# A ninth shared pair of chunks, a fifth weight buffer, and other orders at the ends of chunks, in an attention and mixture-of-experts kernel

## The chip, the cores and the metric

The kernel runs on one core of a Trainium2 chip. The metric is device time in microseconds (us) of one execution. The kernel before was timed three times: 1831.97, 1837.50 and 1835.14, median 1835.14.

## The reference

An attention without softmax over 8 batches of 2496 rows, with a product by `u`, feeds a mixture of eight experts with a gate for each row:

```python
scores = scale * np.matmul(z, z.transpose(0, 2, 1))   # z: 8 x 2496 x 64, scale = 1/2496
attn = np.maximum(scores, 0.0) ** 2
out = np.matmul(attn, v)                              # v: 8 x 2496 x 256
x = (u * out).reshape(19968, 256)
do_compute = x @ w_skip > 0                           # rows that go to an expert
e_idx = np.argmax(xc @ w_gate, axis=1)                # xc = x[do_compute]; 8 experts
h = np.maximum(xc[mask] @ w1[e], 0.0)                 # 256 -> 1024
y[mask] = gate_w[mask, None] * (h @ w2[e])            # 1024 -> 256
out[do_compute] = xc + y                              # all other rows: x
```

Queries and keys are the same `z`, so the matrix `attn` is symmetric.

## The kernel before

**Attention.** The queries of a batch are cut into five chunks c = 0 to 4: four of 512 and one of 448. The keys are cut into ten pairs of blocks p = 0 to 9, 256 keys each; p belongs to the key chunk j = p // 2. A step is one (chunk, p): 8 x 5 x 10 = 400 steps. In a step PE forms the scores of 256 keys against the chunk (L251, three products of two halves that run side by side on 64 rows of the array), ACT takes relu and square into the tile `r` (L290, L291), `high()` rounds `r` to `ah` (L313, on ACT where `on_act` says so, else on DVE), `low()` puts the rest into `al` on DVE (L317), and PE adds `ah`·`vh`, `ah`·`vl`, `al`·`vh` into four accumulators (`attend`, L341): `acc[d][t]` for the two halves d of the 256 columns and the two row halves t. Stages run two steps ahead (`LA = 2`).

**Shared weights.** `PAIRS` names chunk pairs (c, j), c < j. Chunk c computes the weights of j's keys, DVE transposes them in blocks (L268), and SP's queue writes them to memory (`keep`, L686). Chunk j later does not compute the weights of c's keys: SP's queue brings them back (`recall`, L280, issued five steps ahead), and only `high()` and `low()` remain. Such a step is "known" below. Batch 0 leaves out the pairs with c = 0. `ORDER[c]` sets the order of p within a chunk, `EXTRA[c]` which further p have their rounding on ACT.

**The end of a chunk.** In the last step (`k == NP - 1`) the accumulators of d = 0 are finished first; then come the products of the step before for d = 1, and its own. `part(d, 1)` copies `acc[d][1]` on ACT (L369), `part(d, 0)` adds `acc[d][0]` to it on DVE (L371); only then can the next chunk use those buffers, since `ps_acc` has four. `mul` (L374) multiplies by `u`, `turn_rows` (L378) transposes, `store` (L387) writes. After every second chunk `routing` computes logits on PE (`gates`, L409), transposes them (`logits`, L431, L435), picks the expert on DVE (`route`, `counts`), counts places on PE (`place`, L476) and writes each row's entry into its expert's list with an indirect DMA on GpSimd (POOL; `put_in`, L500).

**Loads.** `load_v` and `load_z` bring the next batch's `v` and `z` and split them on ACT and DVE (L119/L120, L108/L109) at steps set by `later(...)`; in the last three chunks `load_w` does it for expert 0.

**Experts.** After the attention each expert's rows run in units of 256. A unit has four `h_part`s (L598, then relu on ACT, L603, and the rest on DVE, L604) and then `y_part`s (L617). `fills` puts other work behind the k-th of these seven parts: 0 to 3 are the `h_part`s, 4 to 6 the `y_part`s. The first unit of expert 0 (its rows were fetched early) carries the routing of the last chunk in its fills: `logits` and `route` behind part 1, `counts` behind 2, `end_routes` (`place` and two `put_in`) behind 3, `end_lists` behind 5.

The order on each engine is that in which the code is written (`manual_schedule`): every engine's queue runs in that order and waits at an instruction whose inputs are not there.

Of the kernel before, what the change touches and what calls it, by code (L numbers as in the profile page):

```python
# [8 lines left out]
F32 = mybir.dt.float32  # L9
# [8 lines left out]
P = 128  # L18
# [7 lines left out]

PAIRS = ((0, 1), (0, 2), (0, 3), (1, 2), (1, 3), (2, 3), (2, 4), (3, 4))
ORDER = (  # L30
# [5 lines left out]
)  # L36
EXTRA = ((8,), (3, 8), (4, 5), (6, 7), (1, 3))


C_TRI, C_REV, C_OFF, C_IDS, C_THR, C_END = 0, 128, 192, 256, 260, 270  # L40
# [7 lines left out]
def attn_moe(ctx, tc, zT, uT, v, wg, w1, w2, cst, pad, out):  # L48
# [113 lines left out]

    def load_u(ci):
        b, q0, n = chunks[ci]
        uts[ci] = xp.tile([P, 2, QC], F32, name="ut", tag="ut", bufs=4)
        nc.sync.dma_start(uts[ci][:, :, :n], uT[b, :, :, q0 : q0 + n])

    warm = cpool.tile([P, 1], F32, name="warm")
# [83 lines left out]
        return ps  # L252

    def r_tile():
        return ap.tile([P, 2, QC], F32, name="r", tag="r", bufs=4)

    turned_r, puts, step = {}, [], [0]

# [135 lines left out]
    def routing(cis, rows64=True):  # L394
# [27 lines left out]
        def logits():  # L422

            ps = psg.pop()
            lgf = lg.rearrange("p t c -> p (t c)")
            same = all(n % P == 0 for n in ns)
            for g, n in [(0, ns[0])] if same else enumerate(ns):
                full = 32 * (n // P)
                w = P * len(ns) if same else P
                o = g * P  # L430
                nc.vector.transpose(lgf[:full, o : o + w], ps[:full, o : o + w])  # L431
                if n % P:
                    k = o + n % P
                    nc.gpsimd.memset(lgf[full : full + 32, k : o + P], 0.0)
                    nc.vector.transpose(lgf[full : full + 32, o:k], ps[full : full + 32, o:k])  # L435

        def route():
# [231 lines left out]
    def at(s, f):  # L669

        todo.setdefault(s // 2, []).append(f)
# [30 lines left out]
    for ci, (b, q0, n) in enumerate(chunks):  # L702
        s0 = ci * NB
        if ci + 1 < NC:
            at(s0 + 12, lambda ci=ci: load_u(ci + 1))
        if ci == 0:
            first = [(4 * j - 8, j % 2, 3, load_z, j) for j in range(2, NZ)]
            first += [(2 * g - 4, 1, 4, load_v, g) for g in range(2, NB // 2)]
            for s1, _, k, load, j in sorted(first, key=lambda x: x[:2]):
                eng = nc.vector  # L710
                if s1 - k < 0:
                    at(s1, load(0, j, eng))
                else:
                    later(s1 - k, k, load, 0, j, eng)
            at(14, lay_pads)
        if q0 == 0 and b + 1 < B:

            end = s0 + NB * -(-S // QC)
            for j in range(NZ):
                s1 = (s0 + 24, s0 + 44, end - 18, end - 14, end - 10)[j]  # L720
                later(s1, 7, load_z, b + 1, j, nc.vector)
            for g in range(NB // 2):
                s1 = s0 + 21 + 8 * g if g < 7 else (end - 17, end - 14, end - 12)[g - 7]
                later(s1, 7, load_v, b + 1, g, nc.vector)

    s_end = NC * NB
    s_w = s_end - 3 * NB

    def start_w():
        for k, f in enumerate(load_w(0, nc.vector)):  # L730
            at(s_w + 8 + 5 * k, f)

    at(s_w, start_w)

# [20 lines left out]
    for s, (ci, p) in enumerate(steps):  # L755
        b, q0, n = chunks[ci]
        k = s % NP
        step[0] = s
        ahead(s + LA + 3)
        if k == 0:  # L760
            accs[ci] = [[ps_acc.tile([P, QC], F32, name="acc", tag="acc") for _ in range(2)] for _ in range(2)]
        acc = accs[ci]
        if k < NP - 1:
            high, low = stage(s + LA)
            high()
            low()
            for d in range(2 if k < NP - 2 else 1):
                attend(b, n, p, d, acc[d], *aa[s], k == 0, False)
            if k < NP - 2:
                aa.pop(s)  # L770
        else:


            part, mul, rows0, rows1, store = finish(ci)
            attend(b, n, p, 0, acc[0], *aa[s], False, True)
            part(0, 1, acc[0])
            part(0, 0, acc[0])
            high, low = stage(s + LA)
            attend(b, n, steps[s - 1][1], 1, acc[1], *aa.pop(s - 1), False, False)
            if s + LA in known:  # L780

                high()
                low()
                high = low = lambda: None
            attend(b, n, p, 1, acc[1], *aa.pop(s), False, True)
            part(1, 1, acc[1])
            high()
            part(1, 0, acc[1])
            low()
            mul()  # L790
            accs.pop(ci)

            new.append(ci)
            if ci < NC - 1:
                after = [(rows0, 2), (rows1, 3), (store, 4), (store, 5)]
                if ci % 2 == 0:
                    gates, logits, route, counts, gate, place, put_in = routing(new)
                    after = [(gates, 2), (logits, 2), (rows0, 2), (rows1, 3), (route, 4), (counts, 4),
                             (store, 4), (gate, 5), (store, 5), (place, 6)]
                    for t in range(0, 4 * len(new), 2):  # L800
                        f = lambda put_in=put_in, t=t: put_in(t, t + 2)
                        if s + 6 + t < len(steps):
                            after.append((f, 6 + t))
                        else:
                            left.append(f)
                    new = []
                for f, k in after:
                    todo.setdefault(s + k, []).append(f)
            else:
                gates, logits, route, counts, gate, place, put_in = routing(new, False)  # L810
        for f in todo.pop(s, []):
            f()
        put_some()
# [57 lines left out]
    for e in range(E):  # L871
# [3 lines left out]
        for i in range(NFIX):  # L875
# [11 lines left out]
            elif i == 0:  # L887
                add(fills, (0, lambda: turn_pe(pair(0, 1), turned(0, 1))))
                add(fills, (0, gates), (0, rows0), (0, rows1), (0, store), (0, store), (1, logits), (1, route),
                    (2, counts), (2, gate), (3, end_routes), (5, end_lists))  # L890
                add(fills, *zip((0, 2), left))
            elif i == 1:
                add(fills, (1, end_counts), (3, lambda: turn_pe(pair(0, 2), turned(0, 2))), (4, rows(0, 3)), (6, rows(0, 4)))
                add(fills, *zip((1, 3, 5), wq[:3]))
            else:
                add(fills, (1, rows(1, 0)), (3, rows(0, 5)), (4, lambda: turn_pe(pair(0, 3), turned(0, 3))),
                    (5, rows(1, 1)), (6, lambda: load_ids(idts[2], 2, 2 * NSTAT)))
                add(fills, *zip((1, 2, 3, 5, 6), wq[3:]))
# [99 lines left out]
```

## Time and profile before

| | |
|---|---|
| median of three runs | 1835.14 us |
| the profiled execution: its own time, and its span | 1834.64 us, 1832.8 us |
| mean granted TensorE clock | 0.996 |
| attention | start to about 1322 us |
| experts | about 1322 us to the end |
| scores: matmuls of 448 columns (L251) | three groups x96 |
| scores: matmuls of 512 columns (L251) | three groups x460 |
| POOL's fill of logits (L434) | x8, 147 to 199 ns |

The span is from the first to the last instruction on the chip; the execution's own time has 1.8 us more around it. In a row of a timeline the first two numbers are the start and the duration in us; what stands in brackets is the idle time of the engine before it and who ended it. A group's row has the busy time in us and the mean ns of one instruction, then the idle time ahead of it.

### The profile page before, as it was taken

How to read it: one execution, taken by the hardware profiler on the slowest of the kernel's cores; microseconds unless marked ns; L12 is line 12 of the kernel's file. 1: busy time of each engine (PE TensorE's matmuls, PEld its weight loads, DVE VectorE, ACT ScalarE, POOL GpSimd, SP SyncE). 2: the span in 40 equal slices, each digit the busy share in tenths (PEclk: the TensorE clock that was granted, in tenths of full speed). 3: DMA queues.
4: the chain of work that ended last, by engine and by line, in shares of the span. 5: the costliest groups of instructions: out<-in, count | busy, mean ns of one | idle time of the engine just before them, and what ended most of it. 6: DMA issues, size and time to landing. Idle time of an engine off the chain costs nothing. (4 is left out here: it accounts for less than half of the span.)

```text
span 1832.8 us, 40463 instructions
## 1 busy us (share of the span) xinstructions
PE 1787.2 (98%) x15844; PEld 1575.9 (86%) x15844; DVE 1182.8 (65%) x2105; ACT 1159.5 (63%) x1499; POOL 440.8 (24%) x429
## 2 busy tenths in 40 slices
PE   8999999999999999999999999999989999999997
PEld 7888878877887798788879878877889999999997
DVE  6777776876777687678678777867643343334432
ACT  8877876877777687678777876877523233333321
POOL 0102201210220120121012022112254556635621
PEclk9999999999999999999999999999989999999999
DMA  5575687487657847784784787578542233313210
GB/s 185 128 179 138 168 207 190 122 207 187 170 136 196 207 116 193 202 198 119 186 215 108 183 208 187 133 182 197 147 103 76 80 96 106 89 53 94 84 37 26
DMA packets 403766, 267.46 MB, mean 146 GB/s; under 512 B 205859, under 2 KB 334117, under 8 KB 403440
## 3 DMA queue, kind: packets, MB, share of 16 engines
q1 hardware_dynamic: 389440, 240.47, 51.9%
q0 software_dynamic: 13712, 22.99, 4.4%
q8 instruction: 141, 2.31, 0.5%
q14 instruction: 185, 1.52, 0.3%
q10 hardware_dynamic: 288, 0.17, 0.0%
HBM read 145.80 MB, written 118.39 MB: 144 GB/s over the span
## 5 line engine op out<-in xcount | busy, mean ns | idle before, releaser
L341 PE MATMUL acc<-ah,vh 64*128 64x512 f32 (+1 forms) x3120 | 729.5, 387 | 17.5 <-DVE xrow L371 11.4
L341 PE MATMUL acc<-ah,vl 64*128 64x512 f32 (+1 forms) x3120 | 712.7, 385 | 0.0
L317 DVE TENSOR_TENSOR al<-r,ah 128x1024 fp32r<-128x1024 f32 (+3 forms) x464 | 480.0, 1048 | 251.1 <-ACT ah L313 238.8
L341 PE MATMUL acc<-al,vh 64*128 64x512 f32 (+1 forms) x3120 | 562.0, 385 | 3.6 <-DVE al L317 3.2
L341 PEld LDWEIGHTS acc<-ah,vh 64*128 64x128 f32 x3120 | 423.8, 185 | 87.4 <-DVE xrow L371 25.8
L341 PEld LDWEIGHTS acc<-ah,vl 64*128 64x128 f32 x3120 | 424.0, 185 | 45.9 <-DVE vl L120 0.2
L500 POOL DMA_INDIRECT lst<-pair,dest x160 | 192.4, 1203 | 1093.4 <-DVE dest L498 996.1
L290 ACT ACTIVATE r<-ps 128x1024 f32<-128x1024 f32 (+1 forms) x278 | 280.3, 1008 | 225.2 <-PE ps L251 185.3
L341 PEld LDWEIGHTS acc<-al,vh 64*128 64x128 f32 x3120 | 361.3, 185 | 58.6 <-DVE al L317 11.9
L313 ACT CAST ah<-r 128x1024 fp32r<-128x1024 f32 (+3 forms) x381 | 329.1, 891 | 37.8 <-DMA r<-kept 13.2
L291 ACT ACTIVATE r<-r 128x1024 f32<-128x1024 f32 (+1 forms) x278 | 289.9, 1043 | 8.8
L603 ACT ACTIVATE hh<-psh 128x512 fp32r<-128x512 f32 (+1 forms) x172 | 98.7, 584 | 293.2 <-PE psh L598 256.7
L617 PE MATMUL y<-w2t,hh 128*128 128x256 f32 x1328 | 246.5, 287 | 0.0
L598 PE MATMUL psh<-xt,w1h 128*128 128x256 f32 (+1 forms) x1280 | 231.8, 284 | 2.1 <-issue 1.8
L617 PEld LDWEIGHTS y<-w2t,hh 128*128 128x128 f32 x1328 | 208.7, 193 | 1.3 <-issue 1.3
L598 PEld LDWEIGHTS psh<-xt,w1h 128*128 128x128 f32 x1280 | 196.9, 189 | 3.1 <-issue 3.1
L604 DVE SCALAR_TENSOR_TENSOR hl<-psh,hh 128x512 fp32r<-128x512 f32 (+1 forms) x172 | 113.0, 671 | 131.6 <-ACT hh L603 126.0
L617 PE MATMUL y<-w2t,hl 128*128 128x256 f32 x664 | 189.0, 285 | 1.2 <-DVE hl L604 1.2
L598 PE MATMUL psh<-xt,w1l 128*128 128x256 f32 (+1 forms) x640 | 181.1, 283 | 0.0
L268 DVE STREAM_TRANSPOSE rt<-r 128x512 f32<-128x512 f32 x244 | 158.4, 687 | 1.2 <-DMA kept<-rt 1.1
L251 PE MATMUL ps<-zh 64*128 64x512 f32 (+1 forms) x556 | 137.8, 399 | 4.6 <-ACT zh L108 4.6
L251 PE MATMUL ps<-zl,zh 64*128 64x512 f32 (+1 forms) x556 | 135.8, 391 | 0.0
(170 smaller groups left out, 1661.1 us busy)
## 6 DMA issues: line engine op xcount, KB each, us to landing
kept<-rt SPq DMA_DIRECT2D x244, 256.0 KB, 4.9
r<-kept SPq DMA_DIRECT2D x488, 128.0 KB, 4.0
raw<-in_v SPq DMA_DIRECT2D x80, 256.0 KB, 3.8
ut<-in_uT SPq DMA_DIRECT2D x32, 512.0 KB, 5.1
xr<-xrow SPq DMA_DIRECT2D x128, 128.0 KB, 3.1
out<-xrow SPq DMA_DIRECT2D x128, 128.0 KB, 3.2
raw<-in_w SPq DMA_DIRECT2D x64, 256.0 KB, 3.3
zf<-in_zT SPq DMA_DIRECT2D x40, 256.0 KB, 3.8
```

What stands on the lines that cost most here:

```text
L251: nc.tensor.matmul(to, k[h, o : o + P], queries(q, h, n), start=(m == 0), stop=(m == 2))
L268: nc.vector.transpose(t[:, :, 32 * k : 32 * k + 32], r[:, x, :].rearrange("p (m i) -> p m i", i=32))
L290: nc.scalar.activation(r[:, :, :n], ps[:, :, :n], AF.Relu, scale=isc)
L291: nc.scalar.activation(r[:, :, :n], r[:, :, :n], AF.Square)
L313: (nc.scalar.copy if on_act(ci, p) else nc.vector.tensor_copy)(h_, r_)
L317: nc.vector.tensor_sub(l_, r_, f32(h_))
L341: nc.tensor.matmul(acc[t][:, :n], w[h, x, dd], a[h, x, :n], start=(first and t not in halves[:m]), stop=(last and t not in halves[m + 1 :]),)
L500: put = nc.gpsimd.indirect_dma_start(out=lst, out_offset=bass.IndirectOffsetOnAxis(ap=dest[:, t : t + 1], axis=0), in_=pair[:, t, :], in_o ...
L598: nc.tensor.matmul(ps[:, j * W : (j + 1) * W], wt[:, a, o : o + P], x[:, d, :W], start=(m == 0), stop=(m == 5),)
L603: nc.scalar.activation(hh[:, : G * W], ps[:, : G * W], AF.Relu)
L604: nc.vector.scalar_tensor_tensor(hl[:, : G * W], ps[:, : G * W], 0.0, f32(hh[:, : G * W]), op0=ALU.max, op1=ALU.subtract)
L617: nc.tensor.matmul(ys[t], h[:, tt], w2t[f][:, k, :], start=(f == 0 and m == 0 and t % 2 == 0), stop=(f == NF - 1 and m == 2), skip_group_c ...
```

## The change

Six things are altered.

1. `PAIRS` gets (1, 4): in each of the 8 batches chunk 1 keeps its weights for the keys of chunk 4 (p = 8, 9), and chunk 4 recalls p = 2, 3. `ORDER` and `EXTRA` of chunks 1 and 4 are new.
2. `r` gets five buffers (was four), `ut` three (was four).
3. In the step before a chunk's last, the rounding of the stage two steps on is put off: where it is on ACT, it comes behind the copy and the sum of d = 0.
4. `load_v` and `load_z` run at steps given in a list; `load_w` too.
5. The fill of logits (L434) is on DVE, not on POOL.
6. In the first unit `end_routes` stands behind part 4 and `end_lists` behind part 6.

```diff
-PAIRS = ((0, 1), (0, 2), (0, 3), (1, 2), (1, 3), (2, 3), (2, 4), (3, 4))
+PAIRS = ((0, 1), (0, 2), (0, 3), (1, 2), (1, 3), (1, 4), (2, 3), (2, 4), (3, 4))
 ORDER = (
     (0, 1, 2, 3, 8, 4, 5, 6, 7, 9),
-    (2, 3, 0, 4, 1, 5, 8, 6, 7, 9),
+    (2, 0, 4, 5, 1, 6, 7, 8, 9, 3),
     (4, 0, 1, 6, 2, 7, 3, 8, 9, 5),
     (6, 0, 2, 1, 8, 3, 9, 4, 5, 7),
-    (0, 1, 2, 3, 4, 5, 6, 7, 8, 9),
+    (0, 2, 1, 3, 4, 8, 5, 6, 7, 9),
 )
-EXTRA = ((8,), (3, 8), (4, 5), (6, 7), (1, 3))
+EXTRA = ((8,), (2, 3), (4, 5), (6, 7), (1,))
...
-        uts[ci] = xp.tile([P, 2, QC], F32, name="ut", tag="ut", bufs=4)
+        uts[ci] = xp.tile([P, 2, QC], F32, name="ut", tag="ut", bufs=3)
...
-        return ap.tile([P, 2, QC], F32, name="r", tag="r", bufs=4)
+        return ap.tile([P, 2, QC], F32, name="r", tag="r", bufs=5)
...
-                    nc.gpsimd.memset(lgf[full : full + 32, k : o + P], 0.0)
+                    nc.vector.memset(lgf[full : full + 32, k : o + P], 0.0)
...
+            jobs = [(load_v, 0, 1, 3), (load_z, 0, 1, 6), (load_v, 1, 2, 3), (load_z, 1, 2, 5), (load_v, 2, 2, 7)]
+            jobs += [(load_v, 3, 3, 3), (load_v, 4, 3, 4), (load_v, 5, 3, 6), (load_v, 6, 3, 7)]
+            jobs += [(load_v, 7, 4, 2), (load_z, 2, 4, 3), (load_v, 8, 4, 4), (load_z, 3, 4, 5)]
+            jobs += [(load_v, 9, 4, 6), (load_z, 4, 4, 7)]
+            for load, j, c, k in jobs:
+                later(s0 + c * NB + 2 * k - 7, 7, load, b + 1, j, nc.vector)
...
-        for k, f in enumerate(load_w(0, nc.vector)):
-            at(s_w + 8 + 5 * k, f)
+        for k, f in zip((4, 6, 12, 14, 16, 22, 24, 26), load_w(0, nc.vector)):
+            at(s_w + 2 * k, f)
...
             high, low = stage(s + LA)
-            high()
-            low()
+            if k < NP - 2 or s + LA in known:
+                high()
+                low()
+                high = low = lambda: None
             for d in range(2 if k < NP - 2 else 1):
                 attend(b, n, p, d, acc[d], *aa[s], k == 0, False)
             if k < NP - 2:
                 aa.pop(s)
+            rest = high, low
         else:
             part, mul, rows0, rows1, store = finish(ci)
             attend(b, n, p, 0, acc[0], *aa[s], False, True)
+            high, low = rest
+            if s + 1 < len(steps) and not on_act(*steps[s + 1]):
+                high()
+                low()
+                high = low = lambda: None
             part(0, 1, acc[0])
             part(0, 0, acc[0])
+            high()
+            low()
             high, low = stage(s + LA)
...
-                    (2, counts), (2, gate), (3, end_routes), (5, end_lists))
+                    (2, counts), (2, gate), (4, end_routes), (6, end_lists))
```

**Where chunk 2 of batch 1 ends and chunk 3 begins.** ACT first, before and then after. `xrow` from `acc` is the copy of a first or second column half (the first of the two rows is d = 0); `ah_3864` and `ah_3899` are the rounding for chunk 3's first step, `ah_3905` and `ah_3912` for its second, a known one.

```order
L290 ACTIVATE r_3861<-ps_3854 128x1024
L291 ACTIVATE r_3861<-r_3861 128x1024
L313 CAST ah_3864<-r_3861 128x1024
L369 COPY xrow_3881<-acc_3442 128x512
L313 CAST ah_3905<-r_3746 128x1024
L369 COPY xrow_3881<-acc_3444 128x512
```

```order
L290 ACTIVATE r_3868<-ps_3861 128x1024
L291 ACTIVATE r_3868<-r_3868 128x1024
L369 COPY xrow_3884<-acc_3453 128x512
L313 CAST ah_3899<-r_3868 128x1024
L313 CAST ah_3912<-r_3757 128x1024
L369 COPY xrow_3884<-acc_3455 128x512
```

The first copy has moved ahead of the first rounding. At the same place on DVE, before and after:

```order
L317 TENSOR_TENSOR al_3865<-r_3861,ah_3864 128x1024
L371 TENSOR_TENSOR xrow_3881<-acc_3441,xrow_3881 128x512
L317 TENSOR_TENSOR al_3906<-r_3746,ah_3905 128x1024
L371 TENSOR_TENSOR xrow_3881<-acc_3443,xrow_3881 128x512
L374 TENSOR_TENSOR ut_3308<-xrow_3881,ut_3308 128x1024
```

```order
L371 TENSOR_TENSOR xrow_3884<-acc_3452,xrow_3884 128x512
L317 TENSOR_TENSOR al_3900<-r_3868,ah_3899 128x1024
L317 TENSOR_TENSOR al_3913<-r_3757,ah_3912 128x1024
L371 TENSOR_TENSOR xrow_3884<-acc_3454,xrow_3884 128x512
L374 TENSOR_TENSOR ut_3315<-xrow_3884,ut_3315 128x1024
```

The first sum is now ahead of both `al`; the second sum is behind both, as before.

**Where chunk 0 of batch 1 ends and chunk 1 begins**, on DVE, before and after (chunk 1's first two steps were both computed; now the second is known):

```order
L313 CAST ah_2924<-r_2921 128x1024
L317 TENSOR_TENSOR al_2925<-r_2921,ah_2924 128x1024
L371 TENSOR_TENSOR xrow_2949<-acc_2492,xrow_2949 128x512
L371 TENSOR_TENSOR xrow_2949<-acc_2494,xrow_2949 128x512
L317 TENSOR_TENSOR al_2994<-r_2968,ah_2993 128x1024
```

```order
L371 TENSOR_TENSOR xrow_2953<-acc_2500,xrow_2953 128x512
L317 TENSOR_TENSOR al_2966<-r_2929,ah_2965 128x1024
L317 TENSOR_TENSOR al_2982<-r_2826,ah_2981 128x1024
L371 TENSOR_TENSOR xrow_2953<-acc_2502,xrow_2953 128x512
L374 TENSOR_TENSOR ut_2373<-xrow_2953,ut_2373 128x1024
```

Here too the second sum has come behind two `al`; before, it stood directly behind the first sum.

**The first unit of the experts**, on PE, before and after: `tri` and `ones` are the two matmuls of `place`, `psh` the last part 3, `y` a `y_part`.

```order
L598 MATMUL psh_18806<-xt0_18289,w1l_17854 128x256
L476 LDWEIGHTS tri_127
L476 MATMUL psm_18821<-hot_18672,tri_127 128x32
L476 LDWEIGHTS ones_129
L476 MATMUL psm_18821<-pre_18673,ones_129 128x32
L617 MATMUL y_18702<-w2t_17984,hh_18703 128x256 x2
```

```order
L617 MATMUL y_18759<-w2t_18107,hh_18760 128x256 x2
L617 MATMUL y_18759<-w2t_18107,hl_18761 128x256
L476 LDWEIGHTS tri_127
L476 MATMUL psm_18890<-hot_18729,tri_127 128x32
L476 LDWEIGHTS ones_129
L476 MATMUL psm_18890<-pre_18730,ones_129 128x32
```

The first `y_part` (12 matmuls) now stands between the last `h_part` and `place`.

More of the change, by code (lines that the diff above doesn't have):

```diff
@@ L716, in attn_moe @@
         if q0 == 0 and b + 1 < B:
[L718 to L724, printed above, removed]
+            jobs = [(load_v, 0, 1, 3), (load_z, 0, 1, 6), (load_v, 1, 2, 3), (load_z, 1, 2, 5), (load_v, 2, 2, 7)]
[4 more added lines that the diff above has]
+                later(s0 + c * NB + 2 * k - 7, 7, load, b + 1, j, nc.vector)
     s_end = NC * NB
```

## The prediction

> **What bounds the kernel now.** I read the page's busy times first, then PE's waits, then the timeline where PE waits longest, then the other engines stretch by stretch.
>
> ```profile
> PE 1787.2 (98%) x15844; PEld 1575.9 (86%) x15844; DVE 1182.8 (65%) x2105; ACT 1159.5 (63%) x1499; POOL 440.8 (24%) x429
> ```
>
> PE is the bound: 45.6 us of the 1832.8 are idle. Time goes away only where PE gets fewer matmuls or waits less. Its waits, with total, times and longest:
>
> ```profile
> PE acc L341 <- DVE xrow L371: 11.4, 15, 1.0
> PE psm L476 <- DVE hot L451: 6.4, 1, 6.4
> PE acc L341 <- ACT xrow L369: 3.3, 7, 0.5
> PE acc L341 <- DVE al L317: 3.2, 12, 0.3
> ```
>
> Rows 1 and 3 are the ends of chunks, where the next chunk waits for its accumulators; row 2 is one wait in the experts' first unit. The rows count only idle time: matmuls overlap, so a late start costs more than it shows here. I take delays from starts instead.
>
> **Part 1: fewer scores.** Chunk 4 recalls p = 2 and 3 in each of 8 batches: 16 calls of 448 columns go.
>
> ```profile
> 304.83 0.36 PE L251 MATMUL ps<-zh 64*128 64x448 f32 x1
> 305.44 0.39 PE L341 MATMUL acc<-ah,vh 64*128 64x512 f32 x1
> ```
>
> A call lasts from its first matmul to the next product's first: 0.61 us, a beat of 0.203 for each of three pairs. 16 x 0.61 = **9.8 us** less for PE. The Trainium skill's page "TensorE: Matmul & The Clock Gate" (Wait — 56ns, not 53.3ns?) gives N / 2.4 GHz + 2.5 ns from start to start, an estimated 0.189 for 448 columns; by it the term would be 9.1 us. The trace does not agree exactly; its beat is 7% longer and is what I use.
>
> What the recall adds lies on other engines: per batch four transposes on DVE, two roundings fewer there, and for each recalled p a rounding and a rest in three pieces.
>
> ```profile
> L268 DVE STREAM_TRANSPOSE rt<-r 128x512 f32<-128x512 f32 x244 | 158.4, 687 | 1.2 <-DMA kept<-rt 1.1
> L290 ACT ACTIVATE r<-ps 128x896 f32<-128x896 f32 x48 | 44.2, 920 | 28.1 <-DVE al L317 16.4 <-PE ps L251 8.3 <-PE psm L516 2.4
> L313 ACT CAST ah<-r 128x384 fp32r<-128x384 f32 x64 | 29.6, 510 | 13.1 <-PE acc L341 8.8 <-DMA r<-kept 4.2
> 964.70:995.00 30.30, 29.65 (x308) 27.85 (x306) 25.18 (x60) 22.13 (x37) 5.39 (x4) 1.00 0.53 143
> 933.40:964.70 31.30, 30.67 (x268) 25.45 (x270) 20.68 (x26) 20.87 (x25) 5.07 (x4) 1.00 0.86 213
> ```
>
> The last two rows are chunks 4 and 3 of batch 5 (length, then busy PE, PEld, DVE, ACT, POOL, clock, DMA share, GB/s). Chunk 1 gains 4 x 0.69 = 2.7 us of DVE. Chunk 4's ACT loses 2 x (0.92 + about 0.95) and gains about as much in pieces of 0.51; its DVE stays at 25.2 us. PE's need there falls from 30.3 to about 29, so DVE comes to 87%: it fits, since in this chunk DVE's work is spread by the loads' new steps, but narrowly. I take the whole 9.8; if DVE held chunk 4 at its length, half (the four batches with routing in it) would be gone. For the fill on DVE the nearest price is POOL's 0.2 us x8, beside PE work.
>
> **Part 2: the first unit.**
>
> ```profile
> 1327.91 0.26 DVE L435 STREAM_TRANSPOSE lg<-psm 32x64 f32<-32x64 f32 x1
> 1328.77 0.28 PE L598 MATMUL psh<-xt,w1l 128*128 128x256 f32 x1
> 1332.94 0.97 POOL L500 DMA_INDIRECT lst<-pair,dest  x1 [0.31 <-issue]
> 1333.88 0.20 POOL L434 MEMSET lg<- 32x64 f32 x1
> 1334.12 0.19 DVE L442 TENSOR_REDUCE mx<-lg 128x4 f32<-128x32 f32 x1 [5.94 <-POOL lg L434]
> 1335.46 0.21 PE L476 MATMUL psm<-hot,tri 128*128 128x32 bf16 x1 [6.41 <-DVE hot L451]
> 1336.86 0.78 PE L617 MATMUL y<-w2t,hh 128*128 128x256 f32 x2
> 1344.55 0.40 PE L617 MATMUL y<-w2t,hh 128*128 128x256 f32 x2
> 1344.91 0.40 PE L598 MATMUL psh<-xt,w1h 128*128 128x256 f32 x2
> 1332.00:1336.00 4.00, 0.21 (x1) 0.13 (x2) 1.68 (x7) 0.71 (x2) 1.78 (x3) 0.50 0.24 46
> ```
>
> The fill, behind the last of a row of indirect DMAs on POOL, holds DVE for 5.94 us, so `hot` is late and `place` stops PE. PE then runs at half clock (last row, 0.50). From the last `h_part`'s end at about 1328.9 to the next unit at 1344.91 are 16.0 us. The 48 `y` matmuls between need 48 x 0.12 = 5.8 (three take the 0.36 us from 1344.55 to 1344.91). With the fill on DVE, `mx` starts at about 1328.3 (1328.17, and 0.1 for the fill). From `mx` to the first matmul of `place` are 1.3 us (1334.12 to 1335.46), from there to the first `y` behind its second 1.4 (1336.86): `hot` is there at 1329.6, `place` through at 1331.1. PE does 12 `y` matmuls until 1330.3, waits 0.8, and ends at 1331.1 + 36 x 0.12 = 1335.5. That is **9.4 us** less. POOL's puts and the list loads also come earlier; nothing of PE waits on them.
>
> The same page (HAM oscillation — how this bites in real kernels) says an idle window of about 3.4 us halves the clock; the trace agrees for these 8 us. By it, 0.8 us would leave the clock up; if the gate closed after all for one window, 1.7 us of the term would go. The term stands on the rows alone.
>
> **Part 3: the ends of chunks.** The end of chunk 2 of batch 5:
>
> ```profile
> 927.55 1.22 DVE L317 TENSOR_TENSOR al<-r,ah 128x1024 fp32r<-128x1024 f32 x1
> 928.82 0.74 PE L341 MATMUL acc<-al,vh 64*128 64x512 f32 x4 [0.30 <-DVE al L317]
> 928.86 1.03 ACT L290 ACTIVATE r<-ps 128x1024 f32<-128x1024 f32 x1 [2.35 <-DVE dest L498]
> 931.01 1.05 ACT L313 CAST ah<-r 128x1024 fp32r<-128x1024 f32 x1
> 931.23 0.82 PE L341 MATMUL acc<-al,vh 64*128 64x512 f32 x4
> 931.96 0.58 ACT L369 COPY xrow<-acc 128x512 f32<-128x512 f32 x1
> 932.59 0.50 PE L341 MATMUL acc<-ah,vh 64*128 64x512 f32 x1 [0.53 <-ACT xrow L369]
> 933.23 0.68 DVE L371 TENSOR_TENSOR xrow<-acc,xrow 128x512 f32<-128x512 f32 x1
> 933.97 0.50 PE L341 MATMUL acc<-ah,vh 64*128 64x512 f32 x1 [0.88 <-DVE xrow L371]
> 934.96 0.69 DVE L371 TENSOR_TENSOR xrow<-acc,xrow 128x512 f32<-128x512 f32 x1
> 935.24 0.96 PE L341 MATMUL acc<-ah,vh 64*128 64x512 f32 x2
> 935.71 0.73 PE L341 MATMUL acc<-ah,vl 64*128 64x512 f32 x2
> ```
>
> The relu at 928.86 waited until the `al` of 927.55 was through: it takes the buffer that this `al` read, though its scores had long been done. Its rounding (931.01) then holds up the copy, the copy the sum. PE's last four products before the end start by 931.66 (932.05 less one duration of 0.39), so with a beat of 0.23 the new chunk is due at 931.9. It starts at 932.59 (0.7 late), goes on at 933.97 instead of 932.82 (1.15), and meets the second sum (934.96 to 935.65), so that 935.24 is followed by 935.71 (0.24 too late). With 0.1 for the restart, 2.2 us go.
>
> After, with T0 the end of the first two accumulators: five buffers let the relu start about 1.8 earlier, so relu and square are done by T0. Copy 0.58, rounding 1.05, two `al` of 1.22 and the second sum 0.69 make 4.8, or 4.6 with their overlaps of 0.1. PE needs the second sum after two steps' remaining products and one of the new: 1.03 + 1.37 + 1.37, less the 0.39 that T0 lies behind the last start: 3.4. So **the second sum becomes the wait**, 1.2 us instead of 2.2: 1.0 less, 8 us in 8 batches. Chunk 1's end has the same chain and waits 1.2 to 1.6 us now: I count nothing, with 0 to 3 as bounds. At chunk 0's end the second sum falls behind two `al` where it had none; PE has 0.7 us of scores more there, so 0.5 us of new wait, 8 x 0.5 = 4 lost (0 to 10 as bounds, from no wait to chunk 2's). Net **4 us** less. The 3.2 us of `al` waits inside chunks: five buffers and the loads' new steps should take about 2 of the later starts behind them, say **3** in all (0 to 6).
>
> **DMA.** 16 more recalls, 8 more kept squares:
>
> ```profile
> kept<-rt SPq DMA_DIRECT2D x244, 256.0 KB, 4.9
> r<-kept SPq DMA_DIRECT2D x488, 128.0 KB, 4.0
> ACT ah L313 <- DMA r<-kept: 13.2, 12, 1.8
> ```
>
> A recall lands in 4.0 us and is issued three steps (about 9 us) ahead of its rounding. At today's rate (13.2 us for 122 recalls, on ACT) 16 add 1.7, and little of it reaches PE: I take 0.
>
> **Sum.** 9.8 + 9.4 + 4 + 3 = 26 us. The profiled execution took 1834.6: 1808.6, and with the median 0.5 above it **1809**.
>
> **The rivals.**
>
> *The ends of chunks gain nothing* (second sums eat all): 1835.1 − 9.8 − 9.4 = 1816. For it: the two `al` ahead of each second sum. Against: the ACT wait of 2.35 is one of buffers. 0.20.
>
> *All chunk-end waits go*, if ACT and DVE overlap better than my chain: 2.2 + 1.4 per batch, 29 in place of 4 + 3: 1787. 0.05.
>
> *The first unit's wait is only replaced*, by `pre` or by `hl` on DVE's queue: 1818. Against: DVE's own rows add up to 1331. 0.07.
>
> *Slower: recalls come late.* Chunk 3 stands at a DMA share of 0.86 (row above, 26.9 of 31.3 us). It gets two recalls and two more loads of `v`, 1.5 MB; at its own 213 GB/s and 0.86 that is 6 us more of the engines: over 1.0. If recalls then land late, ACT's rounding and PE wait. It must cost 26 us, 3.3 per batch, to undo the gain, 4.0 to be slower by 0.3%; 5 per batch gives 1849. The longest such wait now is 1.8. Of the page "DMA: Bandwidth & Descriptors" (Where 436 GB/s comes from) the limit of about 358 GB/s per core speaks against it: 213 plus 1.5 MB in 31 us is 261. The trace shows no more than such rates; where they would end no run here shows. 0.08, half of it slower and half within.
>
> **How the numbers follow.** Forecast 0.60, rivals as given. A measurement of this kernel tells about 0.3%, 5.5 us, from no change. Faster: 0.92; within: 0.04; slower: 0.04. The range reaches up over the first and third rival with parts of chunk 4's loss (1821) and down to 1797, where half of the chunk-end waits go beyond my terms.
>
> **What would show it.** L251's 448-column groups at x48; no wait of `mx` on POOL, PE's wait at `hot` under 1.5 us and full clock there; ACT's relu no longer waiting at the ends of chunks 1 and 2; PE's waits on L371 at d = 1 of chunks 1, 2 and 3, not at d = 0. Wrong would be: PE waits on `ah` behind recalls in chunks 3 and 4, DVE without a gap through chunk 4, or chunk 0's end losing over 1.5 us.

## The result, and the profile after

The changed kernel took **1822.78 us** (median of 4 runs, 1821.36 to 1823.52), the kernel before 1835.03 beside it (4 runs, 1831.97 to 1837.5): ratio 0.9933, 95% interval 0.9916 to 0.995. It is 12.3 us faster, where 26 were forecast. In the profiled executions the attention ends at 1317.5 us in place of 1321.7 (4.2 less); what follows it takes 502.1 in place of 511.1 (9.0 less). So the first unit's term came, and of some 17 us in the attention only a quarter.

The groups by line and shape, after:

```profile
L251 PE MATMUL ps<-zh 64*128 64x448 f32 x64 | 14.9, 368 | 0.0
L268 DVE STREAM_TRANSPOSE rt<-r 128x512 f32<-128x512 f32 x276 | 179.2, 687 | 4.8 <-DMA kept<-rt 4.8
L290 ACT ACTIVATE r<-ps 128x896 f32<-128x896 f32 x32 | 29.3, 916 | 12.0 <-PE ps L251 11.8
L313 ACT CAST ah<-r 128x384 fp32r<-128x384 f32 x96 | 44.5, 511 | 55.1 <-DMA r<-kept 34.8 <-PE ps L251 6.8 <-PE acc L341 6.0
```

The 448-column scores went from 96 to 64: 16 calls of two matmuls for each product. (The prediction looked for x48, a slip of counting; 16 calls fewer are 32 matmuls fewer.) ACT's relu (L290) waited for `al` and `dest` before (total, times, longest):

```profile
ACT r L290 <- DVE al L317: 20.5, 10, 2.4
ACT r L290 <- DVE dest L498: 9.2, 4, 2.4
```

After, neither wait is there. But ACT's rounding (L313) now waits for recalls. ACT's waits for them and PE's waits, after:

```profile
ACT ah L313 <- DMA r<-kept: 99.0, 54, 4.0
```

```profile
PE acc L341 <- DVE xrow L371: 11.0, 15, 0.8
PE acc L341 <- DVE al L317: 9.1, 21, 1.3
PE ps L251 <- ACT zh L108: 4.6, 1, 4.6
PE psm L476 <- DVE pre L457: 4.2, 5, 1.2
PE acc L341 <- DVE ah L313: 4.0, 6, 1.2
```

ACT's wait for recalls was 13.2 us in 12 times, and is 99.0 in 54. On PE the wait at `hot` (6.4) and that for the copy (3.3) are gone; those for `al`, `ah` and `pre` (3.2, 1.5 and 1.2 before) are about three times what they were. How a late recall reaches PE is seen in chunk 4 of batch 4, in the timeline:

```profile
815.10 1.12 ACT L313 CAST ah<-r 128x384 fp32r<-128x384 f32 x3 [1.30 <-DMA r<-kept]
816.13 0.61 ACT L119 CAST vh<-raw 128x512 fp32r<-128x512 f32 x1
816.65 0.91 ACT L290 ACTIVATE r<-ps 128x896 f32<-128x896 f32 x1
817.59 0.95 ACT L291 ACTIVATE r<-r 128x896 f32<-128x896 f32 x1
818.58 0.63 DVE L313 CAST ah<-r 128x896 fp32r<-128x896 f32 x1 [1.10 <-ACT r L291]
819.26 0.47 PE L341 MATMUL acc<-ah,vh 64*128 64x448 f32 x2 [1.18 <-DVE ah L313]
```

Here PE does not wait for the recalled weights; it waits for the next computed step. ACT's queue is in order: the relu of that step (816.65) stands behind a rounding that waited 1.30 us for its recall and behind a split of `v`, so `ah` is there at 819.21, and PE stands for 1.18 us. The stretches of chunks 3 and 4 of batch 4, then of batch 5 (length, busy PE, PEld, DVE, ACT, POOL, clock, DMA share, GB/s):

```profile
761.90:794.30 32.40, 31.45 (x297) 24.87 (x296) 26.41 (x54) 21.08 (x29) 5.29 (x4) 1.00 0.98 238
794.30:823.90 29.60, 28.10 (x266) 25.59 (x264) 20.47 (x37) 20.06 (x34) 4.18 (x4) 1.00 0.89 192
926.90:957.40 30.50, 29.72 (x261) 26.39 (x259) 22.17 (x29) 20.60 (x26) 4.94 (x4) 1.00 0.95 220
957.40:991.30 33.90, 31.32 (x302) 27.45 (x301) 24.58 (x62) 20.76 (x37) 5.33 (x4) 0.95 0.80 191
```

In batch 5 the DMA share was 0.86 in chunk 3 and 0.53 in chunk 4 before. Now it is 0.95 in chunk 3 and 0.80 in chunk 4 (0.98 and 0.89 in batch 4).

For what follows I cut the attention at the end of each chunk, taken as the end of its second copy (L369, d = 1) in the timeline, and add up each chunk over the 8 batches (without the very first chunk, which has the start in it). Us:

| kernel | chunks 0 and 1 | chunk 2 | chunks 3 and 4 | all |
|---|---|---|---|---|
| before | 510.9 | 275.7 | 489.7 | 1276.3 |
| after | 511.1 | 269.9 | 492.4 | 1273.4 |
| e1: no ninth pair | 509.5 | 265.1 | 482.5 | 1257.2 |
| e3: loads' old steps | 513.5 | 274.0 | 485.0 | 1272.5 |
| e4: no store to `out` | 511.5 | 265.0 | 479.1 | 1255.7 |
| e5: neither | 509.6 | 265.0 | 482.6 | 1257.2 |
| e6: e1 with four `r` | 509.9 | 271.6 | 492.6 | 1274.1 |
| e7: e1, old ends of chunks | 509.5 | 263.7 | 486.5 | 1259.7 |
| e8: loads of `v` earlier | 519.2 | 270.4 | 486.9 | 1276.5 |
| e10: kept, not recalled | 511.3 | 270.4 | 487.2 | 1268.9 |
| e11: recalled, not kept | 508.6 | 265.5 | 487.2 | 1261.3 |
| e13: a quarter of the store to `out` | 511.3 | 265.8 | 483.1 | 1260.2 |
| e14: e4, a split of `z` moved | 511.7 | 265.0 | 480.2 | 1256.9 |

(0 and 1, and 3 and 4, stand together because the pair's new orders move one stage of scores from the end of chunks 0 and 3 into chunks 1 and 4. The sums hold to about 0.1 us, single columns to 0.5.)

Where the recalls come late is seen when ACT's wait for them (us) and the DMA share (mean of the eight batches) are taken by chunk:

| kernel | wait in chunks 2, 3, 4 | DMA share in chunks 2, 3, 4 |
|---|---|---|
| before | 0.3, 4.2, 4.2 | 0.77, 0.82, 0.57 |
| after | 44.8, 13.9, 34.8 | 0.86, 0.92, 0.83 |
| e1: no ninth pair | 0, 7.7, 2.5 | 0.78, 0.91, 0.68 |
| e4: no store to `out` | 2.0, 0.8, 12.0 | 0.79, 0.86, 0.67 |
| e10: kept, not recalled | 40.7, 16.1, 0 | 0.86, 0.93, 0.68 |
| e11: recalled, not kept | 23.7, 6.8, 33.3 | 0.77, 0.92, 0.82 |

The pair's writes raise the share in chunk 2, its recalls that in chunk 4. Chunk 3 is as full without the pair, and has the least of the waits.

### The profile page after: what moved, and what is told of

It reads as the page before. It is cut to its first block, busy times and chain, and to the rows that moved or that the text cites. A ratio compares the mean times of both kernels' runs of the same rounds, so it can differ in the third digit from the quotient of the medians.

```text
span 1819.6 us, 40553 instructions
## 1 busy us (share of the span) xinstructions
PE 1774.3 (98%) x15748; PEld 1572.8 (86%) x15748; DVE 1195.9 (66%) x2153; ACT 1161.1 (64%) x1523; POOL 434.1 (24%) x421
## 5 line engine op out<-in xcount | busy, mean ns | idle before, releaser
L341 PE MATMUL acc<-al,vh 64*128 64x512 f32 (+1 forms) x3120 | 568.4, 386 | 9.4 <-DVE al L317 9.1
L341 PEld LDWEIGHTS acc<-ah,vh 64*128 64x128 f32 x3120 | 433.7, 184 | 79.0 <-DVE xrow L371 19.1
L341 PEld LDWEIGHTS acc<-ah,vl 64*128 64x128 f32 x3120 | 433.7, 185 | 43.1 <-DVE vl L120 0.2
L500 POOL DMA_INDIRECT lst<-pair,dest x160 | 186.7, 1167 | 1095.6 <-DVE dest L498 1061.4
L313 ACT CAST ah<-r 128x1024 fp32r<-128x1024 f32 (+2 forms) x437 | 357.9, 847 | 136.6 <-DMA r<-kept 99.0
L290 ACT ACTIVATE r<-ps 128x1024 f32<-128x1024 f32 (+1 forms) x262 | 265.4, 1013 | 124.8 <-PE ps L251 118.2
L291 ACT ACTIVATE r<-r 128x1024 f32<-128x1024 f32 (+1 forms) x262 | 274.6, 1048 | 8.3
L268 DVE STREAM_TRANSPOSE rt<-r 128x512 f32<-128x512 f32 x276 | 179.2, 687 | 4.8 <-DMA kept<-rt 4.8
L251 PE MATMUL ps<-zh 64*128 64x512 f32 (+1 forms) x524 | 128.2, 401 | 4.6 <-ACT zh L108 4.6
L617 PEld LDWEIGHTS y<-w2t,hl 128*128 128x128 f32 x664 | 126.9, 191 | 1.6 <-DVE hl L604 1.6
```

Source lines behind the costliest of these rows:

```text
L251: nc.tensor.matmul(to, k[h, o : o + P], queries(q, h, n), start=(m == 0), stop=(m == 2))
L268: nc.vector.transpose(t[:, :, 32 * k : 32 * k + 32], r[:, x, :].rearrange("p (m i) -> p m i", i=32))
L290: nc.scalar.activation(r[:, :, :n], ps[:, :, :n], AF.Relu, scale=isc)
L291: nc.scalar.activation(r[:, :, :n], r[:, :, :n], AF.Square)
L313: (nc.scalar.copy if on_act(ci, p) else nc.vector.tensor_copy)(h_, r_)
L341: nc.tensor.matmul(acc[t][:, :n], w[h, x, dd], a[h, x, :n], start=(first and t not in halves[:m]), stop=(last and t not in halves[m + 1 :]),)
```

## The experiments

**Without the ninth pair.** The tables of before, all else as changed.

```diff
-PAIRS = (..., (1, 3), (1, 4), (2, 3), (2, 4), (3, 4))
+PAIRS = (..., (1, 3), (2, 3), (2, 4), (3, 4))
```

> The changed kernel with PAIRS, ORDER and EXTRA of before: no ninth pair, all else as changed. Chunk 4 computes p = 2 and 3 again, 9.8 us more matmuls. If the ninth pair gives back more than it saves (late recalls or the new order make PE wait in chunk 4, 17 us more than before over the eight batches), this kernel is faster than the changed one: about 1815 to 1819 against 1822.8. If the pair is worth its 9.8 us and something else ate the gain, it takes about 1832.

1805.41 us, ratio 0.9847 (0.9831 to 0.9864). This version beats both kernels: the pair does not win 9.8 us, it costs 17 by the medians and 16.2 by the chunks. ACT's and PE's waits in it:

```profile
ACT ah L313 <- DMA r<-kept: 12.5, 11, 2.0
```

```profile
PE acc L341 <- DVE xrow L371: 10.3, 15, 0.8
PE ps L251 <- ACT zh L108: 4.6, 1, 4.6
PE acc L341 <- DVE al L317: 2.6, 12, 0.3
```

Chunks 3 and 4 of batch 4 in it:

```profile
756.00:789.00 33.00, 32.05 (x303) 25.37 (x301) 25.62 (x52) 21.80 (x27) 5.29 (x4) 1.00 0.95 216
789.00:816.50 27.50, 27.50 (x272) 25.46 (x270) 21.03 (x35) 21.75 (x34) 4.05 (x4) 1.00 0.73 170
```

Chunk 3 stands at 0.95 here too, and its recalls are in time; what differs most is chunk 4, 0.73 in place of 0.89. So a nearly full chunk 3 alone makes no recall late. That it is borne because chunk 4 has room to catch up is a reading that no run tests.

**The first unit alone.** The kernel before with the fill on DVE and the two fills moved.

```diff
-                    nc.gpsimd.memset(lgf[full : full + 32, k : o + P], 0.0)
+                    nc.vector.memset(lgf[full : full + 32, k : o + P], 0.0)
...
-                    (2, counts), (2, gate), (3, end_routes), (5, end_lists))
+                    (2, counts), (2, gate), (4, end_routes), (6, end_lists))
```

> The kernel before with only the fill on DVE and end_routes and end_lists behind parts 4 and 6. By part 2 of the prediction 9.4 us less than before: 1825.6, with a full clock after the attention. If the first unit's wait is only replaced by another: 1832 or more.

1824.26 us, ratio 0.9954 (0.9937 to 0.997), 8.8 us less than before. The term was 9.4.

**The loads' old steps,** all else as changed.

```diff
...
-            for load, j, c, k in jobs:
-                later(s0 + c * NB + 2 * k - 7, 7, load, b + 1, j, nc.vector)
...
+            for g in range(NB // 2):
+                s1 = s0 + 21 + 8 * g if g < 7 else (end - 17, end - 14, end - 12)[g - 7]
+                later(s1, 7, load_v, b + 1, g, nc.vector)
```

> The changed kernel with load_v and load_z at the steps of before, so that chunk 3 has two loads of v less. Theory late recalls (the DMA engines are full in chunks 3 and 4): DMA share in chunk 3 falls from 0.95 to 0.98 to about 0.9, ACT's wait for recalls from 99 us to about 70, and the time by 2 to 5 us. Theory order (the new order of chunk 4 holds ACT and DVE whatever the DMA does): no gain, 0 to 4 us more, since loads stand at the ends of chunks again.

1825.14 us, ratio 0.9955 (0.9941 to 0.9969): the interval overlaps that of the changed kernel. ACT waits 84.5 us for recalls. The loads' new steps neither cause the lateness nor cure it, and the old ones give no gain, as the second theory had it.

**Without the store of attention rows to `out`.** This takes 20.4 MB off the DMA engines and nothing off PE, ACT and DVE.

```diff
             dst = dsts.pop(0)
+            if dst is out:
+                return
```

> The changed kernel without the store of the attention's rows to the output (rows that go to no expert are not written); the store for the experts' input stays. It takes about 0.15 of the DMA engines' time away. Late recalls: ACT's wait for recalls falls from 99 to under 40 us, PE's waits in chunk 4 go by more than half, 8 us or more less than the changed kernel. Order: ACT waits less for recalls but PE's waits in chunk 4 stay, under 3 us less.

1803.27 us, ratio 0.9836 (0.9819 to 0.9852), 19.5 us less than the changed kernel by the medians, 17.7 by the chunks. ACT's wait for recalls is back at the old size:

```profile
ACT ah L313 <- DMA r<-kept: 15.7, 14, 3.2
```

So the recalls come late for want of DMA time. But with recalls in time the pair wins 1.5 us against e1, not 9.8. The control is e5, which leaves the same store out of e1:

> The kernel without the ninth pair (1805.4), and without the store of the attention's rows to the output: the control for the run of the changed kernel without that store (1803.3, 19.5 less than with it). Theory late recalls: without the ninth pair the DMA engines are not the limit, so leaving the store out changes little, 1802 to 1806; the 19.5 us are then the price of the ninth pair's transfers, and what is left between the two kernels (the pair should win 9.8 and does not) is order and DVE. If the store costs as much here (1788 to 1792), it is a cost of its own and says nothing about recalls.

Ratio 0.9864 (0.9839 to 0.9889), on another chip, where before took 1839.95. Its chunks are those of e1 to 0.1 us: without the pair the store is free. (In the profiled runs of e5, e6, e7 and e8, all on that chip, what follows the attention took 510 to 518 us, against 498 to 504 in every other run with the new first unit, in e5 with one stretch of 5.9 us in which ACT waited for nothing that the records show. So I compare these four by their chunks.)

**Four buffers of `r`, and the old ends of chunks,** both on e1.

```diff
-        return ap.tile([P, 2, QC], F32, name="r", tag="r", bufs=5)
+        return ap.tile([P, 2, QC], F32, name="r", tag="r", bufs=4)
```

> The kernel without the ninth pair (1805.4) with four buffers of r again. If the fifth buffer brought most of the gain at the ends of chunks (relu no longer waits for the rest of the step before): 1815 to 1820, ACT's relu waits on DVE come back. If the copies ahead of the roundings did: 1806 to 1809.

```diff
-            if k < NP - 2 or s + LA in known:
-                high()
-                low()
-                high = low = lambda: None
+            high()
+            low()
...
             part(0, 1, acc[0])
             part(0, 0, acc[0])
-            high()
-            low()
```

> The kernel without the ninth pair (1805.4) with the roundings ahead of the copies again, as before, at every chunk's end. If the order at the ends brought most of the gain: 1814 to 1820, PE's wait for the first sums (d = 0) back. If the fifth buffer alone did: 1806 to 1810.

Ratios 0.9965 (0.9953 to 0.9977) and 0.9853 (0.9827 to 0.9879). The fifth buffer is worth 16.9 us of chunks (1274.1 less 1257.2), a little more than the 10 to 15 that the expectation gave; 10.1 are in chunks 3 and 4. With four, ACT's relu waits on DVE again:

```profile
ACT r L290 <- DVE al L317: 14.1, 8, 2.4
ACT r L290 <- DVE xrow L378: 8.5, 3, 2.8
ACT r L290 <- DVE dest L498: 6.8, 4, 2.3
```

With the old ends the chunks are 2.5 us longer, but 3.4 us stand in the very last chunk alone (32.0 for 28.6, where PE waits 3.4 us for `ut` at L409); the other 38 together are 0.9 shorter, and chunk 2 is 1.4 better. So the sums ahead of the roundings are worth nothing that these runs show, and the fifth buffer brought the gain.

**Loads of `v` taken out of the full chunk.** The changed kernel with the next batch's first seven pieces of `v` in chunks 0 to 2.

```diff
+            if b:
+                jobs = [(load_v, 0, 0, 5), (load_v, 1, 0, 6), (load_v, 2, 0, 7), (load_z, 0, 0, 8), (load_v, 3, 1, 2)]
+                jobs += [(load_v, 4, 1, 4), (load_z, 1, 1, 5), (load_v, 5, 1, 6), (load_v, 6, 2, 3)]
```

> The changed kernel (1822.8) with the loads of v moved out of chunk 3: from batch 1 on, three in chunk 0, three in chunk 1, one in chunk 2, and those of chunk 4 as they are. Nothing of the transfers is left out, they only fall where the DMA share is 0.5 to 0.75. Late recalls: ACT's wait for recalls falls from 99 to under 60 us and the time by 5 to 10 us. Order and DVE: no gain, or slower, since chunks 0 and 1 get the loads' work on DVE and ACT.

Ratio 0.9958 (0.9939 to 0.9976). Chunks 3 and 4 are 5.5 us shorter, chunks 0 and 1 8.1 longer, and ACT still waits 85.9 us for recalls, as the second theory had it. Neither this place nor that of e3 is free.

**Wide recalls,** on the changed kernel and on e1.

```diff
-        src = kept[p // 2, ci % NQ].rearrange("(a k i) q -> a i k q", a=4, k=4)
-        for a in range(4):
-            nc.sync.dma_start(r[32 * a : 32 * a + 32], src[a, :, p % 2 * 2 : p % 2 * 2 + 2, :])
+        src = kept[p // 2, ci % NQ].rearrange("(a k i) q -> k a i q", a=4, k=4)
+        for x in range(2):
+            nc.sync.dma_start(r[:, x, :], src[p % 2 * 2 + x])
```

> The changed kernel with each recall written as 2 transfers of 256 KB in place of 4 of 128 KB: the same bytes, the same packets of 2 KB, half the issues on SP (276 in place of 552). Theory 1 (the time of the 16 DMA engines in chunks 3 and 4 is used up, 0.95 to 0.98 there): nothing moves, ratio to before 0.991 to 0.995, ACT's wait for recalls stays at 80 to 110 us. Theory 2 (it is the number of transfers: SP's queue has few under way at once, and each issue waits for an older one): recalls are issued and land earlier, ACT's wait falls under 40 us, ratio 0.982 to 0.987.

> The changed kernel with the pairs and orders of before (no ninth pair), and recalls in 2 transfers of 256 KB. Theory 1 (DMA time decides): as without the ninth pair, ratio 0.983 to 0.987. Theory 2 (the number of transfers decides): below that, 0.978 to 0.982.

2138.92 us (ratio 1.167, 1.1653 to 1.1688) and 2041.34 (1.1138, 1.1119 to 1.1157): neither theory, and no answer to the question. ACT's and PE's waits in the first:

```profile
ACT ah L313 <- DMA r<-kept: 490.7, 154, 9.0
```

```profile
PE acc L341 <- ACT ah L313: 134.7, 78, 3.8
PE acc L341 <- ACT xrow L369: 33.6, 19, 3.2
```

The bytes and the packets of 2 KB are the same. The records of single packets show why: while a wide recall runs, 4 packets of 2 KB are under way at a time, and 16 to 18 while a load of `u` does (around 885 us). The form of the access put each of them on four engines. The Trainium skill's page "DMA: Bandwidth & Descriptors" (Why a DMA increments its semaphore by 16 and not by 1) has the rule: a transfer runs on the largest number up to 16 that divides the slowest dimension of both sides. Here these are 4 and 128, so 4, and the trace agrees.

**The pair's two halves.** First, chunk 1 keeps, chunk 4 computes all the same; second, chunk 4 recalls (from what chunk 2 kept), chunk 1 keeps nothing for it.

```diff
-            if (p // 2, ci % NQ) in pairs(ci // NQ):
+            if (p // 2, ci % NQ) in pairs(ci // NQ) and (p // 2, ci % NQ) != (1, 4):
```

> The changed kernel with chunk 1 keeping its weights for chunk 4 as in the change, but chunk 4 not bringing them back: it computes p = 2 and 3 itself (16 score calls of 448 columns more, 9.8 us of PE). Theory 1 (the recalls' transfers in the full chunks 3 and 4 are what costs): ACT's wait for recalls falls under 35 us and the kernel is faster than the changed one in spite of the 9.8 us: ratio 0.984 to 0.988. Theory 2 (the keeping costs: transposes, the new order and the writes in chunk 1): ratio 0.996 to 1.0.

```diff
-        old, new = r, (ci % NQ, p // 2) in pairs(b)
+        old, new = r, (ci % NQ, p // 2) in pairs(b) and (ci % NQ, p // 2) != (1, 4)
...
-        src = kept[p // 2, ci % NQ].rearrange("(a k i) q -> a i k q", a=4, k=4)
+        src = kept[p // 2 + (p // 2 == 1 and ci % NQ == 4), ci % NQ].rearrange("(a k i) q -> a i k q", a=4, k=4)
```

> The changed kernel with chunk 4 bringing back p = 2 and 3 from the place that chunk 2 kept for p = 4 and 5 (the same shapes and bytes, other data), and chunk 1 keeping nothing for it: 32 writes of 256 KB and 64 transposes fewer. Weights of p = 2 and 3 of chunk 4 are thus not the right ones. Theory 1 (the recalls cost): about as the changed kernel, ratio 0.989 to 0.994, ACT's wait over 60 us. Theory 2 (the keeping costs): ratio 0.980 to 0.985.

1813.53 us (0.9888, 0.9869 to 0.9907) and 1808.83 (0.9873, 0.9854 to 0.9893), with 61.2 and 64.7 us of ACT's wait. Both lie between what the two theories gave, since each half costs. Against e1, keeping adds 11.7 us of chunks. (That is 32 transposes, not the 64 that the expectation of the second names.) Recalling adds 4.1 though 9.8 of scores are gone, so it costs 13.9. Together 25.6; the changed kernel stands 16.2 above e1, which with the 9.8 is 26.0. The costs add up, though both runs carry the new orders, so that what these cost stands in both.

By chunks, keeping costs 5.3 us in chunk 2 (270.4 for 265.1), where ACT waits 40.7 us for recalls. In the changed kernel the pair's last squares are written as chunk 2 begins, and the recalls behind them in SP's queue go out later: in batch 4 the next one 2.5 us into chunk 2, in e1 the recall at the same place 1.8 us ahead of it, in e4 0.1 us into it. Another 4.2 us are lost in chunk 4 of the odd batches, where no recall is late; what differs from e1 there is the new order of chunk 4.

**Bytes or the number of transfers.** All stores to `out` issued, with a quarter of the rows:

```diff
+            w = nm if dsts else 4
...
-                    dst[t0 : t0 + n, 64 * a : 64 * a + 64].rearrange("(m i) e -> i m e", i=32),
-                    xrow[32 * a : 32 * a + 32, :nm, :],
+                    dst[t0 : t0 + 32 * w, 64 * a : 64 * a + 64].rearrange("(m i) e -> i m e", i=32),
+                    xrow[32 * a : 32 * a + 32, :w, :],
```

> The changed kernel with every store of attention rows to out still issued, at its place and with its waits, but with 128 rows of a chunk in place of 512 or 448: a quarter of the bytes and of the packets, as many transfers on SP's queue. The output lacks the other rows where no expert writes them. Theory 1 (bytes and packets fill the DMA engines): near the run without this store, ratio 0.983 to 0.987, ACT's wait for recalls 15 to 40 us, attention over at 1300 to 1304 us. Theory 2 (the number of transfers on SP's queue): near the changed kernel, ratio 0.990 to 0.995, ACT's wait over 70 us.

1810.43 us, ratio 0.9878 (0.9857 to 0.99), a little above both the range and the wait of theory 1 (ACT waits 55.7 us), and below those of theory 2. Leaving out the whole store takes 17.7 us off the chunks (1273.4 to 1255.7). This run, with as many transfers and 15.2 of the 20.4 MB gone (three quarters), takes off 13.2, three quarters as well. It is the bytes and packets, which went together here, and not the number of transfers.

**Where the pair's 9.8 us go when recalls are in time.** In e4, chunk 4 of batch 5, at the routing that runs there (lines behind the store stand two further down than in the changed kernel):

```profile
963.28 1.34 DVE L459 TENSOR_TENSOR pre<-pre,hot 128x8 bf16<-128x8 bf16 x7
965.17 0.68 DVE L109 TENSOR_TENSOR zl<-zf,zh 128x512 fp32r<-128x512 f32 x1
965.78 1.22 DVE L317 TENSOR_TENSOR al<-r,ah 128x384 fp32r<-128x384 f32 x3
967.05 0.68 PE L341 MATMUL acc<-al,vh 64*128 64x448 f32 x4 [0.78 <-DVE al L317]
```

Routing and a split of `z` stand ahead of an `al`, and PE waits 0.78 us. (The 1.16 us of the expectation below are the wait of PE's weight load at the same place.) e14 is e4 with that split in chunk 3:

```diff
-            jobs += [(load_v, 3, 3, 3), (load_v, 4, 3, 4), (load_v, 5, 3, 6), (load_v, 6, 3, 7)]
-            jobs += [(load_v, 7, 4, 2), (load_z, 2, 4, 3), (load_v, 8, 4, 4), (load_z, 3, 4, 5)]
+            jobs += [(load_v, 3, 3, 3), (load_v, 4, 3, 4), (load_z, 2, 3, 5), (load_v, 5, 3, 6), (load_v, 6, 3, 7)]
+            jobs += [(load_v, 7, 4, 2), (load_v, 8, 4, 4), (load_z, 3, 4, 5)]
```

> The changed kernel without the store of attention rows to out (whose output is incomplete in the same way as before), and with the load and split of the third piece of z moved from chunk 4 to chunk 3. Theory 1 (in chunk 4 of the odd batches VectorE is the bound: routing and two splits stand ahead of an al, and PE waits 1.16 us there and 0.38 us later): one split of 0.69 us gone from there takes 0.5 to 1.1 us off each of these four chunks, 30.0 to about 29.2 us, and attention ends 2 to 4 us earlier, at 1295.5 to 1298 us. Theory 2 (the al waits for ACT's rounding or for the order of the known steps): chunk 4 stays at 30.0 us, attention ends at 1299 to 1301 us.

1805.55 us, ratio 0.9846 (0.9826 to 0.9867), no better than e4; the attention ends at 1300.9 us, where theory 2 had put it (e4: 1299.7). That wait went from 0.78 to 0.38:

```profile
967.71 0.67 PE L341 MATMUL acc<-al,vh 64*128 64x448 f32 x4 [0.38 <-DVE al L317]
```

In three of four odd batches chunk 4 takes 29.6 us in place of 30.0, and the even batches give it back (chunk 3 is 0.3 longer, chunk 4 up to 0.4). So work ahead of the `al` on VectorE's queue is the reason for this wait, and the split is half of it; that routing, which was not moved, is the other half is argued and not shown. The gain in chunk 4, 0.4 us, is below the 0.5 to 1.1 of theory 1.

## Why the prediction was wrong

**The bound and the method held.** Time went only where PE got fewer matmuls or waited less.

**Part 2 held.** 9.4 us were forecast, e2 shows 8.8 and the traces' stretch behind the attention 9.0. The steps are where they were put, after:

```profile
1323.71 0.11 DVE L434 MEMSET lg<- 32x64 f32 x1
1324.12 0.19 DVE L442 TENSOR_REDUCE mx<-lg 128x4 f32<-128x32 f32 x1
1324.63 0.39 PE L617 MATMUL y<-w2t,hh 128*128 128x256 f32 x2
1326.06 0.19 PE L476 MATMUL psm<-hot,tri 128*128 128x32 bf16 x1
1326.86 0.18 PE L476 MATMUL psm<-pre,ones 128*128 128x32 bf16 x1 [0.61 <-DVE pre L457]
1331.27 0.40 PE L598 MATMUL psh<-xt,w1h 128*128 128x256 f32 x2
```

The first `y` product starts at 1324.63 and the next unit at 1331.27: 6.6 us, as worked out (1328.9 to 1335.5), with a wait of 0.61 at `place`.

**The step that failed is the term under "DMA".** It took "today's rate" of ACT's wait, 13.2 us for 122 recalls, for the 16 new ones and ended with "I take 0"; the runs show 17.7 us. The step carried the wait per recall of a kernel with DMA shares of 0.77, 0.82 and 0.57 in chunks 2, 3 and 4 into one where they are 0.86, 0.92 and 0.83, and it gave the 8 new kept squares, which it names, no price at all. What speaks from the runs: ACT's wait of 99.0 us, and 17.7 us of chunks that go with the store's bytes (e4, e13) and only where the pair is (e5). Of these, 13.0 are in chunk 4 and 4.9 in chunk 2; chunk 3 is as long with the store as without it (251.3 and 251.1).

The rival *recalls come late* had the mechanism right and got 0.08. Its place was wrong: it worked out chunk 3, which reached 0.90 to 0.98 in batches 1 to 7 and not the 1.05 of its sum, and lost nothing, while chunk 2 (the writes) and chunk 4 (the recalls) paid. Its price of 3.3 to 5 us per batch was too high (17.7 / 8 = 2.2), so the kernel stayed faster.

**Part 1's own 9.8 us came by half at most.** The bound that I had written down and set aside, half gone "if DVE held chunk 4 at its length", is what e4 shows: against e1, chunks 3 and 4 gain 3.8 us in the even batches (4.9 was the term) and lose 0.4 in the odd ones, where the routing is. Reading DVE's share (87%) as "fits" missed that its work stands in one block ahead of an `al`; a chunk's mean says nothing of that. The wait of 0.78 us shown above is part of these odd batches' loss of 1.3 us each; where the rest goes was not tried. Chunks 0 and 1 lose another 2.0 (509.5 to 511.5); the prediction had put 4 on the new order at chunk 0's end, which comes with the pair. Net 1.5 us.

**Part 3 was too small, by its place.** Without the 4 for chunk 0's end, whose order e1 does not have, it stood at 11 us. Before to e1 the chunks are 19.1 shorter: 10.6 in chunk 2 (8 forecast at its ends), 7.2 in chunks 3 and 4, for which only a part of 3 stood, 1.4 in chunks 0 and 1. The mechanism, buffers of `r` that `al` holds, is shown by e6: 16.9 of the 19.1. I priced it at one end of one chunk and did not look for it in chunk 4, where it is 1.7 us in each odd batch, with routing ahead of `al` on DVE, and 0.7 in most of the even ones (e6 against e1). The new wait was sized right. The end of chunk 2 of batch 5, after:

```profile
924.50 0.57 ACT L369 COPY xrow<-acc 128x512 f32<-128x512 f32 x1
925.10 0.69 DVE L371 TENSOR_TENSOR xrow<-acc,xrow 128x512 f32<-128x512 f32 x1 [0.94 <-ACT xrow L369]
926.05 2.36 DVE L317 TENSOR_TENSOR al<-r,ah 128x1024 fp32r<-128x1024 f32 x2 [0.26 <-ACT ah L313]
926.48 0.55 PE L341 MATMUL acc<-ah,vh 64*128 64x512 f32 x2
927.90 0.39 PE L341 MATMUL acc<-ah,vh 64*128 64x512 f32 x1
928.33 0.68 DVE L371 TENSOR_TENSOR xrow<-acc,xrow 128x512 f32<-128x512 f32 x1
929.07 0.50 PE L341 MATMUL acc<-ah,vh 64*128 64x512 f32 x1 [0.78 <-DVE xrow L371]
```

The first copy and sum (924.50, 925.10) run at once, and the new chunk starts with its products for d = 0 at 926.48 without a wait. Its products for d = 1 start at 927.90, and the second sum behind two `al` (928.33) then costs 929.07 − 927.90 − 0.23 = 0.9 us (1.2 forecast). The rounding that was put off brings nothing by itself (e7).

**The sum.** Unit −9.0, buffers and ends −19.1, the pair −1.5, late recalls +17.7: −11.9, and the medians differ by 12.3. Forecast were −9.4, −11, −5.8 (9.8 less the 4 of chunk 0's end) and 0. That the forecast missed by 14 us and not by 22 is luck: Part 3 brought 8 us more than it said, while late recalls took 17.7 that stood at 0 and the pair fell short by 4.3.

**Still open:** how the 11.7 us of keeping alone (e10) divide. Its 8.4 MB of writes, its 32 transposes and the new orders of chunks 1 and 4 came together in that run and were not tried apart; that 5.3 us fall in chunk 2 and 4.2 in chunk 4 of the odd batches says where, not why. Nor was the routing moved away from the `al` behind it.

## What to carry to other kernels

Where a change trades work of the bound engine for transfers, work out the DMA share of the very stretches that get them, for the writes as well as for the reads (here chunk 2, 0.78 to 0.86, and chunk 4, 0.68 to 0.83): a wait per transfer taken from the emptier kernel no longer holds there, and an in-order engine that handles arrivals passes the delay on to work that has nothing to do with them. A mean share of an engine does not say that work fits: look for the blocks ahead of what the bound engine needs. And try the parts of a bundled change apart, since here one part gave back most of what another won.

## What the hardware showed

- **How full the DMA engines ran.** The share reaches 0.98 at 238 GB/s over a chunk with this mix (packets of 256 B take 19 ns on average, of 512 B 32 ns, of 2 KB 133 ns in the records between 800 and 1100 us of the changed kernel). The limit that I had weighed against late recalls was never near. Nor does the share alone tell whether recalls are late: ACT waited 7.7 us for them in e1's chunk 3 at 0.91, and 44.8 us in the changed kernel's chunk 2 at 0.86.
- **The clock falls after less than a full window without work.** After, in two neighbouring stretches of 3.4 us in chunk 4 of batch 5:

```profile
975.80:979.20 3.40, 1.28 (x12) 0.91 (x13) 3.03 (x12) 2.11 (x6) 0.00 (x0) 1.00 1.08 255
979.20:982.60 3.40, 3.40 (x20) 3.04 (x20) 3.19 (x13) 1.35 (x4) 0.00 (x0) 0.50 0.78 162
```

```profile
979.01 0.97 PE L341 MATMUL acc<-al,vh 64*128 64x448 f32 x4 [1.29 <-DVE al L317]
```

  PE was busy for 1.28 of the 3.40 us ahead, its longest pause 1.29 us (a late `al`), and the clock was at half for the next 3.4. The Trainium skill's page "TensorE: Matmul & The Clock Gate" (What's actually happening) has it at half after an idle window of about 3.4 us; this trace differs, since 38% of work did not keep it up. The wide recalls (e9) show it many times over: all 44 stretches at half clock begin on one grid of 3.41 us. Of the spans of that grid at full clock between 14 and 1640 us, all 23 in which PE was busy for less than 40% were followed by half clock, 20 of the 39 with 40 to 60%, and none of the 356 above (busy time as the profile models it).
- **Same bytes, a sixth more time.** Two ways to write one recall differ by 316 us in this kernel (1822.78 and 2138.92, ratios to before 0.9933 and 1.167), with 4 packets of a recall under way at a time in the slower one.
